# One rounding moved to ScalarE, a transpose of row maxima moved ahead of a score product, and a weight load moved to the end of its slot

## The chip, the cores and the metric

The kernel runs on one core of one Trainium2 chip. The metric is the device time of one execution in microseconds. A profiled execution also has a span, from the first to the last instruction of the program; times of the trace are counted from the start of that span.

## The reference

Attention with a decay, and behind it a soft mixture of experts. All numbers are float32.

```
q, k, v: (8 batches, 8 heads, 576, 64)   f: (8, 8, 576)
scores = q k^T / 8 + cum_i - cum_j,  cum = cumsum(log(clip(f)))
scores above the diagonal = -1e9;  scores -= max over the row
attn = exp(scores) / (sum + 1e-9);  x = attn v  -> (4608 tokens, 512)

logits = x phi (512 x 32);  d = softmax of logits over the tokens
slot_input = d^T x (32 x 512);  per expert (4 slots): relu(. w1[e]) w2[e]
out = softmax of logits over the slots @ slot_out   -> (4608, 512)
```

## The kernel before

**Heads and pairs.** The 64 heads are worked off in 32 pairs. Pair g has a slot of its own in the loop over g (lines 725 to 868). Its heads are h0 = 2g and h1 = 2g + 1. Four slots make a batch; w = (g - 4) mod 4 says which part of the soft-MoE work of an earlier batch a slot carries beside its own: logits behind slot w = 0, their exponentials and transposes in w = 1, the dispatch product and the first part of the combine weights in w = 2.

**Two passes over the scores.** Pass one (`s1`, L230, and `tops`, L243 to L249) computes scores with the query on the partitions, in float32r, in six products of a head (numbers 0 to 5) that lie in four banks. VectorE takes the maximum of every row from them into the tile `MT`: it reads the bank, adds the causal mask, and a second short instruction writes the maximum. Three PSUM banks rotate among these products. When all ten rows of a pair are in `MT`, `mturn` (L256) transposes them on TensorE into a free corner of the bank `pv[0]`, `mrows` copies them on ScalarE to a small tile `mr` (L265) and a DMA on SP's queue puts them as one more row into the rounded queries `YA` (L268). Pass two (`s2`, L283 and L284) computes the scores again with the key on the partitions, the row of maxima being part of the contraction. It is two products for each bank: the rounded operands `WA` and `YA`, and the rests of the rounding, `WB` and `YB`. ScalarE takes the exponential (`expo`, L290), GpSimd zeroes what lies above the diagonal (`causal`, L298 and L301), and `s3` (L315) multiplies with the values into `pv`. `norm` (L330 to L335) divides.

**Operands.** `load_qk` (L174) brings queries and keys of a pair to `RAW` (three buffers), `round_k` and `round_q` (L183, L188) round them on ScalarE into `WA` and `YA` (three buffers), `dup_k` and `dup_q` (L199, L203) copy the rounded ones by DMA into the other half of the partitions of `WB` and `YB` (two buffers), and GpSimd subtracts (`low_k` L209, `low_q` L214). `load_cum` (L194) brings two rows of cumulated decays into `WA`. `wload` (L128) loads one block of 512 KB of expert weights that stays in SBUF until the end.

**The slot.** In slot g, pass two works on pair g, while pass one works on head u0 = 2g + 3 (the second of pair g + 1) in the first half and u1 = 2g + 4 (the first of pair g + 2) in the second. So `MT` of pair g + 1 is complete once the maxima of u0's product 5 are in. The order on every engine is written out by hand: an engine takes its instructions in the order in which the program names them. In the second half of a slot that order is: `px` and `xcopy` of the fifth token block of pair g - 1 (a transposed output, copied from `pv[1]` on ScalarE, L372, two instructions), products 2 and 3 of u1 with their maxima, `s2` and `expo` of h1's banks 1 and 2, `mturn`, `mrows`, then the rest of pass one and two. SP's queue in a slot is: `load_qk`, `load_v`, `wload` (slots 2 to 28), the row of maxima, `load_cum`, `dup_q`, `dup_k`.

**The opening.** Lines 515 to 675 start pairs 0 and 1 by hand, with single products for pass one (`first`) and banks of pass two (`both`) interleaved. There one rounding, the queries of head 3, is made by VectorE (L625). `turner` is an identity; `warm` is a filler product on the constants. L578 is a memset on GpSimd of 64 columns of `YA` that the last product of a head's pass one reads.

```python
71  SIDES = [[x for n in zip(units(h, 0, range(4)), units(h, 1, range(4))) for x in n] ...]
256     nc.tensor.transpose(pm[0 : NBLK * (h1 - h0), 0:128].bitcast(F32R), MT[g % 3][...], turner)
265     nc.scalar.copy(mr[0:n], st["pm", g, h0][0:n, 0:128])
268     nc.sync.dma_start(dst.bitcast(F32), mr[0:n].bitcast(F32))
625 nc.vector.tensor_copy(YA[1][0:64, 1, 64:640], RAW[1][0:64, 1])
736 if 2 <= g < NRES + 2: wload(g - 2)
```

Of the kernel before, what the change touches and what calls it, by code (L numbers as in the profile page):

```python
# [20 lines left out]
NG = B * NPAIR  # L21
# [54 lines left out]
def attn_softmoe(ctx: ExitStack, tc: tile.TileContext, qk, v, f, phi, w1, w2, cst, out):  # L76
# [49 lines left out]
    def wload(n):  # L126
        i, q = divmod(ORDER[n], 4)
        nc.sync.dma_start(quarter[n], (w1, w2)[i % 2][i // 2][:, QW * q : QW * q + QW])  # L128
# [51 lines left out]
    def round_k(g, *hs):  # L180
        if pair(g):
            for h in hs or range(2):
                nc.scalar.copy(WA[g % 3][0:64, S * h : S * h + S], RAW[g % 3][64:128, h])  # L183

    def round_q(g, *hs):
        if pair(g):
            for h in hs or range(2):
                nc.scalar.copy(YA[g % 3][0:64, h, 64:640], RAW[g % 3][0:64, h])  # L188
# [45 lines left out]
    def tops(i, *which):  # L234
        if not head(i):
            return
        g, h = divmod(i, 2)
        for n in which:
            bank, o, blk, j0, w = TOPS[n]
            t = st["top", i % 2, bank]  # L240
            m0 = max(448 - (128 * blk + 64) + j0, 0)
            top = MT[g % 3][:, NBLK * h + blk : NBLK * h + blk + 1] if g else m2[h][:, blk, 1:2]
            if n == 2:  # L243
                nc.vector.tensor_reduce(top, t[:, o : o + w], axis=AX.X, op=ALU.max)  # L244
                continue
            nc.vector.tensor_tensor_reduce(  # L246
                out=t[:, o : o + w], in0=t[:, o : o + w], in1=mask[:, m0 : m0 + w], scale=1.0, scalar=top.bitcast(F32) if n == 3 else -3.0e38,
                op0=ALU.add, op1=ALU.max, accum_out=top,
            )  # L249

    def mturn(g, h0=0, h1=2):

        if not pair(g):
            return
        pm = pv[h0 and 1][:, 384:512]
        nc.tensor.transpose(pm[0 : NBLK * (h1 - h0), 0:128].bitcast(F32R), MT[g % 3][:, NBLK * h0 : NBLK * h1], turner)  # L256
        st["pm", g, h0] = pm
# [29 lines left out]
    def expo(i, bank):  # L287
        if head(i):
            t, at = st["bank"]
            nc.scalar.activation(PT[i % 2][:, SEG_O[bank] : SEG_O[bank] + at], t[:, 0:at], AF.Exp, scale=0.125)  # L290
# [20 lines left out]
    def s3(g, todo):  # L311
        for h, t, u, c in todo:
            r = queries(t, u)
            at = pt_col(c, 64 * r)
            nc.tensor.matmul(  # L315
                pvv[h][64 * u : 64 * u + 64, t, :], PT[h][:, at : at + 64], V[:, g % 2, c, 65 * h : 65 * h + 65], start=(c == 0), stop=(c == r // 2)
            )
# [47 lines left out]
    def xcopy(g, ts):  # L365
        if pair(g):
            n, o = TURN[ts[0]]
            to = XT[g % NPAIR]
            if ts == (4,):
                for h in range(2):  # L370
                    r = slice(64 * h, 64 * h + 64)
                    nc.scalar.copy(to[r, 128:192], pv[n][r, o + 64 * h : o + 64 * h + 64])  # L372
            elif ts == (0, 3):
                to = to[:, 0:384].rearrange("p (n c) -> p n c", c=192)[:, :, 0:128]
                nc.scalar.copy(to, pv[n][:, o : o + 256].rearrange("p (n c) -> p n c", c=128))
            else:
                nc.scalar.copy(to[:, PLACE[ts[0]] : PLACE[ts[0]] + 128 * len(ts)], pv[n][:, o : o + 128 * len(ts)])
# [221 lines left out]
    def first(i, n, busy=0):  # L599
        s1(i, *GROUPS[n])  # L600
        warm(busy, cs)
        tops(i, *GROUPS[n])

    def both(i, n):
        s2(i, *((0,), (1,), (2,), (3, 4, 5))[n])
        expo(i, n)
# [15 lines left out]
    both(0, 1)  # L622
    first(2, 0)
    both(0, 2)
    nc.vector.tensor_copy(YA[1][0:64, 1, 64:640], RAW[1][0:64, 1])  # L625
    next(r1)
    first(2, 1)
    next(r1)
    s2(0, 3, 4, 5)
    round_k(1, 1)  # L630
    expo(0, 3)
    dup_q(1, 1, 2)
    dup_k(1, 1, 2)
# [18 lines left out]
    first(3, 2)  # L652
    first(3, 3)
    round_k(2, 0)
    both(1, 3)
    causal(1)
    low_k(3)
    low_q(3)
    round_q(2, 0)
    s3(0, SIDES[0])  # L660
    mturn(1, 1, 2)
    mrows(1, 1, 2)
    first(4, 0)
    round_k(2, 1)
    round_q(2, 1)
    dup_q(2)
    dup_k(2)
    s3(0, LAST[0])
    norm(0)
    first(4, 1)  # L670
    s3(0, LAST[1] + SIDES[1][:8])
# [53 lines left out]
    for g in range(1, NG):  # L725
        h0, h1 = 2 * g, 2 * g + 1
        u0, u1 = h0 + 3, h0 + 4
        b, w = divmod(g - 4, NPAIR)
        c = b - 1 if w == 0 else b if (b, w) == (B - 2, 3) else None
        if g < 4:  # L730
            load_v(g + 1)
            load_qk(g + 3)
        else:
            load_qk(g + 3)
            load_v(g + 1)
        if 2 <= g < NRES + 2:
            wload(g - 2)
        if w == 1:
            weigh(b)
        low_q(h0 + 2)  # L740
        low_q(h1 + 2)
        s2(h0, 0)
        expo(h0, 0)
        norm(h0 - 1)
        if w == 1:
            mgroup(b)
        if w == 2:
            combine(b, 0)
        s1(u0, 2)
        tops(u0, 2)  # L750
        s2(h0, 1)
        expo(h0, 1)
        s1(u0, 3)
        tops(u0, 3)
        if 1 < g < NG - 1:
            px(g - 1, 0)
        s2(h0, 2)
        expo(h0, 2)
        if g == NG - 1:
            px(g - 1, 0)  # L760
        if g > 1:
            px(g - 1, 3)
        else:
            round_k(3, 0)
            round_q(3, 0)
        s1(u0, 0, 1)
        tops(u0, 0, 1)
        if g > 1:
            px(g - 1, 1)
        s2(h0, 3)  # L770
        if g > 1:
            xcopy(g - 1, (0, 3))
            px(g - 1, 2)
            xcopy(g - 1, (1, 2))
        s2(h0, 4)
        s1(u0, 4, 5)
        s2(h0, 5)
        expo(h0, 3)
        tops(u0, 4, 5)
        causal(h0)  # L780
        low_k(h0 + 2)
        if w == 1:
            mtop(b)
        s2(h1, 0)
        expo(h1, 0)
        if g == 1:
            for t in (0, 3, 1, 2):
                px(0, t)
        px(g - 1, 4)
        if g == 1:  # L790
            xcopy(0, (0, 3))
            xcopy(0, (1, 2))
        xcopy(g - 1, (4,))
        s1(u1, 2)
        tops(u1, 2)
        s2(h1, 1)
        expo(h1, 1)
        s1(u1, 3)
        tops(u1, 3)
        s2(h1, 2)  # L800
        if g < NG - 2:
            expo(h1, 2)
        mturn(g + 1)
        mrows(g + 1)
        if g >= NG - 2:
            expo(h1, 2)
        s1(u1, 0, 1)
        tops(u1, 0, 1)
        s2(h1, 3, 4)
        s1(u1, 4, 5)  # L810
        s2(h1, 5)
        expo(h1, 3)
        tops(u1, 4, 5)
        causal(h1)
        low_k(h1 + 2)
        if g == 1:
            round_k(3, 1)
            round_q(3, 1)
        load_cum(g + 3)
        dup_q(g + 2)  # L820
        dup_k(g + 2)
        if g == 29:
            sides[2].close()
            p2 = fresh(ctx, "p2", 2)
            wstream(*p2, RAW[30 % 3])
        if g == 30:
            sides[1].close()
            xp = ctx.enter_context(tc.tile_pool(name="xp", bufs=1))
            X.append(xp.tile([P, NBLK, 256], F32, name="X3"))
            p0 = fresh(ctx, "p0", 1)  # L830
            p1 = fresh(late, "p1", 3)
            wstream(*p0, *p1, RAW[31 % 3])
        if g == 31:
            sides[0].close()
            with tc.using_default_side("right"):
                tp = ctx.enter_context(tc.tile_pool(name="tp", bufs=1))
            cT = tp.tile([P, sum(CUT)], F32R, name="cT")
            wstream(tp.tile([P, QW], F32, name="w36"))
        if w == 1:
            mcast(b)  # L840
        if c is not None:
            combine(c, 1)
        if w == 2 and b < B - 2:
            dispatch(b, *range(NBLK))
        if g == NG - 1:
            st["lg", B - 1] = scratch(False, f"lg{B - 1}")
            nc.vector.memset(st["lg", B - 1][:, 128:192], -1.0e30)
        round_k(g + 3)
        if w == 1:
            weigh2(b)  # L850
            total(b)
        round_q(g + 3)
        if c is not None:
            combine(c, 2)
        s3(g, VALUES[:30])
        norm(h0)
        if g == 31:
            logits(B - 1, 0, 1)
            wstream(XTS[:, 0:QW], PTS[:, 0:QW])
            split(0, 0)  # L860
            split(1, 0)
        s3(g, VALUES[30:])
        if w == 0:
            logits(b, *range(NPAIR))
        if w == 1:
            tokens(b, 0, 1)
        if g == 28:
            wstream(RAW[29 % 3])
# [272 lines left out]
```

## Time and profile before

| | us |
|---|---|
| median of 3 runs | 391.46 |
| lowest and highest run | 390.41, 395.79 |
| profiled execution | 392.3 |
| its span | 390.6 |
| TensorE busy (matmuls) | 370.5, 95% |
| VectorE, ScalarE, GpSimd busy | 281.7, 271.3, 255.0 |

The profiled execution is 1.7 us longer than its span. TensorE's granted clock, over the whole span, was 0.984 of full speed. Busy matmul time is modelled from pipelined instructions, so ends of matmuls overlap; distances between their starts are read instead. A row of the timeline gives start, duration, engine, line, operation, tiles, and in brackets the idle time before it with what ended it; instructions that follow one another and are alike are merged (xN). A matrix product in float32 shows as two matmul records, one in float32r as one.

### The profile page before, as it was taken

Reading aid. Unit: us, or ns where it says so; the run is one execution under the profiler, and the core shown is the slowest. Engines: PE = TensorE matmul, PEld = TensorE weight load, DVE = VectorE, ACT = ScalarE, POOL = GpSimd, SP = SyncE. Lnnn points to the kernel's source line nnn. Section 1 sums busy time; section 2 is a strip of 40 time slices with the busy share of each in tenths; the row PEclk is TensorE's granted clock in tenths of the full one; section 3 lists DMA queues with packets and bytes.
Section 4 is the critical chain, followed back from the end, with each engine's and each line's share of the span. In section 5 each row is a group of like instructions: output and inputs, shape, how many; then the busy total and the mean of one; then the engine's idle time right before and its main releaser. Section 6 shows DMA issues by size and latency. Waiting matters only on the chain.

```text
span 390.6 us, 15123 instructions
## 1 busy us (share of the span) xinstructions
PE 370.5 (95%) x5863; PEld 330.7 (85%) x5863; DVE 281.7 (72%) x1080; ACT 271.3 (69%) x669; POOL 255.0 (65%) x357
## 2 busy tenths in 40 slices
PE   7999999999999999999999999999999998999870
PEld 7789999999999999999999999999999885567640
DVE  7978887878887788788878887878787534341681
ACT  8869887878787778787878787878786553021560
POOL 4897887878787878787878787878787821000000
PEclk9999999999999999999999999999999998999995
DMA  6875978777777777777777777777775899995798
GB/s 205 205 195 148 283 223 278 189 233 207 224 211 215 213 212 214 213 214 211 213 214 214 211 214 212 214 214 212 212 227 154 269 350 377 407 417 206 264 393 314
DMA packets 34344, 93.72 MB, mean 240 GB/s; under 512 B 4266, under 2 KB 8288, under 8 KB 34272
## 3 DMA queue, kind: packets, MB, share of 16 engines
q1 hardware_dynamic: 34272, 92.75, 76.4%
q8 instruction: 46, 0.75, 0.8%
q14 instruction: 26, 0.21, 0.2%
HBM read 63.93 MB, written 9.73 MB: 189 GB/s over the span
## 4 chain that ended last, share of the span: by engine, by line
PE 86%; DMA 6%; POOL 2%; DVE 1%; ACT 1%; issue 1%; POOLq 0%; DVEq 0%; ACTq 0%
PE pv L315 24%; PE ring L283 14%; PE s L230 13%; PE ring L284 13%; PE pv L342 5%; PE pv L981 4%; PE more L941 4%; PE lg L389 3%; DMA out<-RAW 3%; PE ds L475 2%; DMA YA<-mr 2%; DMA WB<-WA 1%; POOL WB L209 1%; DMA PTS<-in_f 1%; POOL YB L214 1%
## 5 line engine op out<-in xcount | busy, mean ns | idle before, releaser
L290 ACT ACTIVATE PTS<-ring 128x320 f32<-128x320 f32 (+2 forms) x256 | 118.1, 502 | 49.3 <-PE ring L284 36.4
L283 PE MATMUL ring<-YA,WA 67*128 67x320 f32 (+9 forms) x384 | 121.5, 330 | 0.8 <-DMA YA<-mr 0.8
L246 DVE CUSTOM_DVE_ANT_0 s<-s,mask 128x320 f32<-128x320 f32 (+3 forms) x256 | 109.0, 442 | 5.6 <-PE s L230 1.1
L284 PE MATMUL ring<-YB,WB 128*128 128x320 f32 (+4 forms) x384 | 110.4, 296 | 0.0
L315 PE MATMUL pv<-V,PTS 128*64 128x65 f32 x3200 | 101.9, 223 | 0.2 <-POOL WB L209 0.2
L315 PEld LDWEIGHTS pv<-V,PTS 128*64 128x64 f32 x3200 | 96.9, 138 | 3.1 <-issue 1.5
L230 PE MATMUL s<-WA,YA 66*128 66x288 f32 (+9 forms) x384 | 98.2, 310 | 0.8 <-DMA RAW<-in_qk 0.4
L209 POOL TENSOR_TENSOR WB<-RAW,WB 64x576 fp32r<-64x576 f32 x64 | 90.4, 1412 | 11.1 <-DMA WB<-WA 5.8
L214 POOL TENSOR_TENSOR YB<-RAW,YA 64x576 fp32r<-64x576 f32 x64 | 89.7, 1421 | 2.6 <-POOL EX L397 0.2
L283 PEld LDWEIGHTS ring<-YA,WA 67*128 67x128 f32 (+3 forms) x384 | 69.7, 183 | 6.3 <-issue 2.1
L284 PEld LDWEIGHTS ring<-YB,WB 128*128 128x128 f32 (+1 forms) x384 | 70.0, 182 | 0.1
L230 PEld LDWEIGHTS s<-WA,YA 66*128 66x128 f32 (+1 forms) x384 | 62.9, 190 | 7.4 <-ACT PTS L290 1.5
L301 POOL TENSOR_SCALAR_AFFINE_SELECT PTS<-PTS 128x128 f32<-128x128 f32 (+1 forms) x128 | 31.5, 268 | 21.1 <-ACT PTS L290 18.6
L246 DVE DVE_READ_ACCUMULATOR2_ANT MT<- 128x1 fp32r x310 | 43.8, 141 | 0.0
L298 POOL TENSOR_SCALAR_AFFINE_SELECT PTS<-PTS 128x384 f32<-128x384 f32 x64 | 33.5, 523 | 14.2 <-ACT PTS L290 10.3
L342 PE MATMUL pv<-cs,X 128*128 128x128 f32 x155 | 42.0, 277 | 0.0
L183 ACT CAST WA<-RAW 64x576 fp32r<-64x576 f32 x64 | 40.1, 668 | 1.0 <-DMA RAW<-in_qk 0.2
L188 ACT CAST YA<-RAW 64x576 fp32r<-64x576 f32 x63 | 39.6, 671 | 0.4
L246 DVE CUSTOM_DVE_ANT_0 s<-s,mask,MT 128x288 f32<-128x288 f32 x62 | 32.6, 526 | 9.3 <-PE s L230 0.4
L330 DVE TENSOR_SCALAR rl<-pv 128x5 f32<-128x5 f32 x64 | 10.5, 164 | 34.0 <-PE pv L315 23.6
L335 DVE TENSOR_TENSOR X<-pv,rl 128x320 f32<-128x320 f32 (+1 forms) x65 | 31.5, 486 | 2.4 <-DMA YA<-mr 0.3
L244 DVE TENSOR_REDUCE MT<-s 128x1 fp32r<-128x288 f32 x62 | 27.8, 449 | 0.4 <-PE s L230 0.4
(221 smaller groups left out, 389.2 us busy)
## 6 DMA issues: line engine op xcount, KB each, us to landing
w<-in_w SPq DMA_DIRECT2D x45, 512.0 KB
RAW<-in_qk SPq DMA_DIRECT2D x31, 576.0 KB
V<-in_v SPq DMA_DIRECT2D x32, 325.0 KB
YB<-YA SPq DMA_DIRECT2D x30, 288.0 KB
WB<-WA SPq DMA_DIRECT2D x30, 288.0 KB
p<-in_w SPq DMA_DIRECT2D x6, 512.0 KB
out<-RAW SPq DMA_DIRECT2D x6, 512.0 KB
out<-p SPq DMA_DIRECT2D x5, 512.0 KB
```

The source lines that it names most:

```text
L183: nc.scalar.copy(WA[g % 3][0:64, S * h : S * h + S], RAW[g % 3][64:128, h])
L188: nc.scalar.copy(YA[g % 3][0:64, h, 64:640], RAW[g % 3][0:64, h])
L209: nc.gpsimd.tensor_tensor(t[0:64], RAW[g % 3][64:128, h], t[64:128].bitcast(F32), op=ALU.subtract)
L214: nc.gpsimd.tensor_tensor(YB[g % 2][64:128, h], RAW[g % 3][0:64, h], YA[g % 3][0:64, h, 64:640].bitcast(F32), op=ALU.subtract)
L230: nc.tensor.matmul(t[:, o : o + w], ya[0:m, h, 128 * blk : 128 * blk + 128], wa[0:m, j0 : j0 + w], start=True, stop=True)
L246: nc.vector.tensor_tensor_reduce(out=t[:, o : o + w], in0=t[:, o : o + w], in1=mask[:, m0 : m0 + w], scale=1.0, scalar=top.bitcast(F32) if ...
L283: nc.tensor.matmul(o, wa[0:m, j0 : j0 + n], ya[0:m, h, 64 + i0 : 64 + i0 + w], start=True, stop=False)
L284: nc.tensor.matmul(o, wb[:, j0 : j0 + n], yb[:, h, i0 : i0 + w], start=False, stop=True)
L290: nc.scalar.activation(PT[i % 2][:, SEG_O[bank] : SEG_O[bank] + at], t[:, 0:at], AF.Exp, scale=0.125)
L298: nc.gpsimd.affine_select(d3, d3, pattern=[[0, 3], [1, 128]], compare_op=ALU.is_ge, fill=0.0, base=0, channel_multiplier=-1)
L315: nc.tensor.matmul(pvv[h][64 * u : 64 * u + 64, t, :], PT[h][:, at : at + 64], V[:, g % 2, c, 65 * h : 65 * h + 65], start=(c == 0), stop= ...
L342: nc.tensor.transpose(pm[:, 0:128], x[:, t, 128 * (p % 2) : 128 * (p % 2) + 128], ident)
```

## The change

1. In the opening, the rounding of head 3's queries moves from VectorE (L625) to ScalarE, as `round_q(1, 1)` behind `round_k(1, 1)` and ahead of an exponential.
2. In the opening, `round_q(2, 0)` moves on ScalarE ahead of the exponential of `both(1, 3)`. `first(4, 0)` moves ahead of the transposed maxima of head 3. The list `SIDES[0]` is cut at entry 20.
3. In the slots g > 1, `mturn` and `mrows` move ahead of `s2(h1, 2)` and its exponential. The copy of the fifth token block on ScalarE moves from behind `px` to behind `mrows`.
4. `wload` moves from the start of a slot, behind `load_qk` and `load_v`, to its end, behind `dup_q` and `dup_k`.

```diff
@@ opening
     both(0, 2)
-    nc.vector.tensor_copy(YA[1][0:64, 1, 64:640], RAW[1][0:64, 1])
     next(r1)
...
     round_k(1, 1)
+    round_q(1, 1)
     expo(0, 3)
...
     round_k(2, 0)
+    round_q(2, 0)
     both(1, 3)
     causal(1)
     low_k(3)
     low_q(3)
-    round_q(2, 0)
-    s3(0, SIDES[0])
+    s3(0, SIDES[0][:20])
+    first(4, 0)
     mturn(1, 1, 2)
     mrows(1, 1, 2)
-    first(4, 0)
...
-    s3(0, LAST[0])
+    s3(0, SIDES[0][20:] + LAST[0])
@@ slot g
-        if 2 <= g < NRES + 2:
-            wload(g - 2)
...
-        xcopy(g - 1, (4,))
+        if g == 1:
+            xcopy(0, (4,))
         s1(u1, 2)
         tops(u1, 2)
         s2(h1, 1)
         expo(h1, 1)
         s1(u1, 3)
         tops(u1, 3)
+        if g > 1:
+            mturn(g + 1)
+            mrows(g + 1)
+            xcopy(g - 1, (4,))
         s2(h1, 2)
-        if g < NG - 2:
-            expo(h1, 2)
-        mturn(g + 1)
-        mrows(g + 1)
-        if g >= NG - 2:
-            expo(h1, 2)
+        expo(h1, 2)
+        if g == 1:
+            mturn(g + 1)
+            mrows(g + 1)
         s1(u1, 0, 1)
...
         dup_q(g + 2)
         dup_k(g + 2)
+        if 2 <= g < NRES + 2:
+            wload(g - 2)
```

## Rows read from the trace of the kernel before

**Rows 1.** Page, part 1: busy time, share of the span, instructions.

```profile
PE 370.5 (95%) x5863; PEld 330.7 (85%) x5863; DVE 281.7 (72%) x1080; ACT 271.3 (69%) x669; POOL 255.0 (65%) x357
```

**Rows 2.** Stretches: length, busy time of PE, PEld, DVE, ACT, POOL, clock, DMA share, GB/s.

```profile
35.57:121.00 85.43, 85.36 (x1450) 80.47 (x1447) 67.87 (x270) 68.96 (x170) 70.74 (x96) 1.00 0.77 223
130.30:303.60 173.30, 173.09 (x2936) 162.31 (x2937) 138.99 (x556) 136.19 (x341) 139.09 (x191) 1.00 0.74 213
```

**Rows 3.** Waits of TensorE: total us, times, longest.

```profile
PE ring L283 <- DMA YA<-mr: 0.8, 2, 0.5
```

**Rows 4.** Chain of waits, 109 to 131 us: start, us, what.

```profile
126.45 3.80 DMA YA<-mr
```

**Rows 5.** Timeline of VectorE, the opening.

```profile
6.52 0.46 DVE L557 CAST PTS<-PTS 64x576 fp32r<-64x576 f32 x1
...
15.43 1.32 DVE L625 CAST YA<-RAW 64x576 fp32r<-64x576 f32 x1
...
18.61 0.14 DVE L246 DVE_READ_ACCUMULATOR2_ANT MT<- 128x1 fp32r x1
```

**Rows 6.** Timeline of TensorE, the opening.

```profile
16.94 0.30 PE L230 MATMUL s<-WA,YA 66*128 66x64 f32 x1 [0.37 <-DMA RAW<-in_qk]
...
18.13 0.49 PE L511 MATMUL ring<-cs 128*128 128x192 f32 x2
18.89 0.22 PE L256 MATMUL pv<-turner,MT 128*5 128x128 f32 x1 [0.28 <-POOL WB L209]
```

**Rows 7.** Timeline of GpSimd, the opening.

```profile
15.01 1.42 POOL L214 TENSOR_TENSOR YB<-RAW,YA 64x576 fp32r<-64x576 f32 x1
16.49 0.54 POOL L578 MEMSET YA<- 64x128 f32 x2
```

**Rows 8.** Timeline of ScalarE, the opening.

```profile
16.09 0.67 ACT L183 CAST WA<-RAW 64x576 fp32r<-64x576 f32 x1
...
17.82 0.94 ACT L290 ACTIVATE PTS<-ring 128x448 f32<-128x448 f32 x2 [0.57 <-ACT PTS L290]
```

**Rows 9.** Timeline of VectorE: last maximum of u0 in slots 6, 11 and 26.

```profile
76.62 0.14 DVE L246 DVE_READ_ACCUMULATOR2_ANT MT<- 128x1 fp32r x1
...
124.86 0.14 DVE L246 DVE_READ_ACCUMULATOR2_ANT MT<- 128x1 fp32r x1
...
269.50 0.14 DVE L246 DVE_READ_ACCUMULATOR2_ANT MT<- 128x1 fp32r x1
```

**Rows 10.** Timeline of TensorE: h1's bank 2 in the same slots, and a transpose.

```profile
76.62 0.31 PE L283 MATMUL ring<-YA,WA 98*128 98x320 f32 x1
...
125.07 0.31 PE L283 MATMUL ring<-YA,WA 67*128 67x320 f32 x1
...
269.40 0.31 PE L283 MATMUL ring<-YA,WA 67*128 67x320 f32 x1
269.55 0.31 PE L284 MATMUL ring<-YB,WB 128*128 128x320 f32 x1
269.70 0.23 PE L256 MATMUL pv<-turner,MT 128*10 128x128 f32 x1
```

**Rows 11.** Timeline of ScalarE, slot 11, around the copy of the maxima.

```profile
125.10 0.42 ACT L372 COPY XTS<-pv 64x64 f32<-64x64 f32 x2
125.54 0.77 ACT L290 ACTIVATE PTS<-ring 128x320 f32<-128x320 f32 x2
126.19 0.24 ACT L265 CAST mr<-pv 10x128 fp32r<-10x128 f32 x1
```

**Rows 12.** Timeline of SP's queue: two loads of queries and keys.

```profile
38.37 0.39 SPq L174 DMA_DIRECT2D RAW<-in_qk  x1
...
54.09 0.54 SPq L174 DMA_DIRECT2D RAW<-in_qk  x1
```

**Rows 13.** Timeline of ScalarE: the roundings of those loads, and what follows one.

```profile
42.21 1.24 ACT L183 CAST WA<-RAW 64x576 fp32r<-64x576 f32 x2 [0.18 <-DMA RAW<-in_qk]
...
45.08 0.87 ACT L290 ACTIVATE PTS<-ring 128x448 f32<-128x448 f32 x2 [0.37 <-PE ring L284]
...
59.60 1.24 ACT L183 CAST WA<-RAW 64x576 fp32r<-64x576 f32 x2
```

## The prediction

> **What bounds the kernel now.** I read the page's busy times first: TensorE is busy for 95% of the span, the next engine for 72% [rows 1]. An average may hide a stage with room, so next come the stretches: in 35.57 to 121 us TensorE is busy for 85.36 of 85.43 us, in 130.3 to 303.6 us for 173.09 of 173.30, at full clock, while the DMA engines are at three quarters [rows 2]. In the slots, then, a wait of another engine is worth nothing, and one put on TensorE is paid in full. Third, TensorE's list of waits: for the row of maxima it waits twice, 0.8 us together, the longer 0.5 [rows 3]; the chain of waits shows that one behind a DMA which took 3.80 us from its issue in slot 11 [rows 4]. Outside the opening and the tail, 0.8 us is all that an earlier row of maxima can win. The rest had to be found in the order of single instructions, so the timelines of the opening and of the slots' middles come last.
>
> **Part 1 and 2, the opening.** VectorE's copy takes 1.32 us, and its maxima go on behind it, until the last one of head 2 is written at 18.75 (18.61 + 0.14) [rows 5]. TensorE's transpose of these maxima starts at 18.89, behind two fillers from 18.13, after 0.28 us of idle time [rows 6]. The page puts that to GpSimd, but the maxima, written 0.14 us before, explain it as well and are what the transpose reads. Ends of matmuls are modelled: 0.31 us long records follow each other at 0.15 in a stream [rows 10], so the real stall is nearer 0.28 + 0.16 = 0.44. Without the copy the maxima come up to 1.3 us sooner, bounded by the 64-column product at 16.94 (its end 17.24 plus a maximum, under 18.0), and the stall goes: -0.44. ScalarE pays 0.67 for it, behind the rounding at 16.09; its idle 0.57 before 17.82 takes most [rows 8], 0.10 is passed on to the exponentials, whose banks the filler product reuses. Next is the wait at 16.94, 0.37 us [rows 6]: the memset of the columns that this product reads runs from 16.49 on GpSimd, which is in a row of subtractions that the change doesn't touch [rows 7]. It stays.
> I take -0.4. The ends: -0.8 if the 0.37 goes too, +0.7 if the whole rounding on ScalarE shows.
> `round_q(2, 0)` ahead of an exponential delays that by 0.67; the values product that needs it stands 20 entries later, so 0. The list cut at 20 has just 20 entries: nothing moves between its parts. Only `first(4, 0)` and the transpose change places; both are TensorE's and both needed, 0.
>
> On the port the Trainium skill speaks too ("GPSIMD Engine Reference", Specifications): GpSimd shares its SBUF interface with VectorE, and contends with two-port VectorE modes. By it the copy would have slowed GpSimd, and removing it would bring the memset sooner. The trace shows VectorE slowed (1.32 us, where a like cast at 6.52 took 0.46 [rows 5]), but GpSimd's subtraction beside it not (1.42 us [rows 7]). That is rival 2.
>
> **Part 3, the transpose one product sooner.** What it wins: in slot 11 the copy of the maxima starts at 126.19 on ScalarE, behind two copies of the fifth block (from 125.10) and two exponentials (from 125.54) [rows 11]. With the block copies and one exponential behind it, it starts some 0.6 sooner (0.44 by the copies, the rest by the exponential). The DMA's 3.80 us then end 0.6 earlier and the 0.5 wait is gone: -0.5. The other wait (0.3) is in slot 30, where the same edit costs as much (below).
> What it costs: TensorE works in its program's order, so a transpose that has to wait for VectorE holds all behind it. Before, `s2(h1, 2)` covered that. In slot 26 the last maximum is written at 269.64 (269.50 + 0.14) [rows 9], and the transpose starts at 269.70, 0.06 later [rows 10]: just ready, with no idle time. In the new order it would stand where `s2(h1, 2)` starts now, at 269.40, and still can't start before 269.70: a stall of 0.30. In slot 6 the maximum is there at 76.76, plus 0.06 against a place at 76.62: 0.20. Slot 11 is an ordinary one: 125.00 + 0.06 against 125.07: 0.00 [rows 9, 10]. Which slots are which follows from VectorE's queue: in w = 2 `combine` step 0 (L495, L496) stands ahead of the maxima and makes them late. These are slots 6, 10, 14, 18, 22 and 26: 0.20 + 5 x 0.30 = +1.7. The late 0.3 isn't won back: from there to the slot's end the chain holds nothing but TensorE.
> In the 22 ordinary slots the transpose is ready just at its place; the weight load behind it may come later: between 0 and 0.06 each, 0 to +1.3. I take 0.01 each, +0.2, as the transposes that are just ready now show no idle time. Slot 30 is a w = 2 slot too: +0.3 and the wait of 0.3 fall together, 0.
> The exponential of h1's bank 2 moves behind one maxima copy (0.24) and the block copies (0.42) and no longer behind those ahead of it: about 0.4 later. `causal(h1)` needs it, and GpSimd is busy with `low_k` until then; cover gone, 0.4 late at the values product's second half, which starts 1.2 us after the first. 0.
>
> **Part 4, the weights.** SP's issue of 0.4 us is passed by nothing urgent: the row of maxima waits for ScalarE, not for SP. What changes is the order of the data: 512 KB now stand ahead of the queries and keys of the same slot (26 loads) instead of behind. At 223 GB/s for a share of 0.77 [rows 2] a full queue moves 290 GB/s, and 512 KB are 1.8 us. The only rounding that waited for its load began 3.8 us after the issue (38.37 to 42.21); the shortest other distance I found is 5.5 us (54.09 to 59.60) [rows 12, 13]. 3.8 + 1.8 = 5.6: 0.1 us late in one slot, under ScalarE's idle 0.37 behind such roundings [rows 13]. I take 0; the ends are 0 and rival 3.
>
> **Sum.** -0.4 - 0.5 + 1.7 + 0.2 = +1.0 us. The profiled execution, 392.3 us (span 390.6 and 1.7 around it), would become 393.3; it stands 0.8 above the median of 391.46, which becomes **392.5 us**. With the ends of the terms that case spans 391.1 (opening -0.8, ordinary slots 0) to 394.7 (opening +0.7, ordinary slots +1.3).
>
> **Rivals.**
> 1. The transposes don't stall. VectorE's maxima would have to come 0.3 us sooner in the w = 2 slots. For: a VectorE that waits for TensorE elsewhere could catch up when the opening gives it time. Against: the same delay in slots 10 to 26, and nothing taken from VectorE's slots. Then -0.4 - 0.5 and 0: 390.6 us.
> 2. GpSimd's port: without the copy the memset comes sooner by the 0.37 that TensorE waits. Against: the subtraction of 1.42. Then +0.6: 392.1 us.
> 3. Slower: the queries and keys behind the weights come late, ScalarE stands at `round_k` with the next slot's exponentials behind it, and TensorE runs out of free banks. It decides where a load takes over 5.5 - 1.8 = 3.7 us now; the one measured took 3.8 at most. If landing in a full queue takes 2 us more than that, some ten slots wait 0.5 or so past ScalarE's idle time: +5, 397.5 us. All 26 by 0.5 or more: +13, 405 us. For: one rounding waits already. Against: one only, of 32.
> 4. The change does nothing that shows: the transpose is late whenever it could help, and the stalls and gains cancel: 391.5 us.
>
> **How the numbers follow.** My forecast 0.5; rival 1 0.2; rival 2 0.05; rival 3 0.15, of which 0.03 beyond 2%; rival 4 0.1. The runs before spread over 1.4%, so 2% (7.8 us) is about what can be told from no change: faster 0.01, within 2% 0.95, slower 0.04. The range reaches from rival 1 to the upper end of the forecast and the low part of rival 3: 390.0 to 395.0.
>
> **What would show it.** Right: TensorE waits for VectorE at L256 in slots 6 to 26 of w = 2, some 0.3 each; those slots 0.3 longer, the others unchanged; no wait for the row of maxima in slot 11; slot 2 starts 0.4 earlier than 35.57 [rows 2]. Wrong: ScalarE waiting at L183 for a DMA in many slots, no wait at L256, or a slot 2 that starts later.

## The result

Over 22 runs each, taken in the same rounds, the kernel before had a median of 390.94 us (389.62 to 395.97) and the changed one 393.42 us (393.04 to 395.36). The ratio is 1.0079, with a 95% interval of 1.0066 to 1.0092: the change costs 2.6 to 3.6 us, about 3.1. The ratio is of fast runs alone and so leaves out two slow ones of the kernel before, 395.79 and 395.97; the medians of all runs are 2.48 apart. The forecast was 392.5 us in a range of 390.0 to 395.0, by a sum of +1.0 us. The time lies in the range and on the forecast's side; the cost is about three times the sum.

### The profile page after: what moved, and what is told of

It is laid out like the page before. It is cut to its first block, busy times and chain, and to the rows that moved or that the text cites. A ratio compares the mean times of both kernels' runs of the same rounds, so it can differ in the third digit from the quotient of the medians.

```text
span 391.5 us, 15170 instructions
## 1 busy us (share of the span) xinstructions
PE 371.3 (95%) x5863; PEld 329.3 (84%) x5863; DVE 281.2 (72%) x1079; ACT 275.4 (70%) x670; POOL 254.8 (65%) x357
## 4 chain that ended last, share of the span: by engine, by line
PE 75%; DVE 9%; ACT 6%; DMA 5%; issue 2%; POOL 0%; SPq 0%; ACTq 0%; DVEq 0%; POOLq 0%
PE pv L315 21%; PE ring L283 12%; PE ring L284 10%; PE s L230 10%; DVE s L246 4%; PE pv L342 4%; PE pv L984 4%; PE more L944 4%; PE lg L389 3%; DMA out<-RAW 3%; PE ds L475 2%; ACT WA L183 2%; ACT YA L188 2%; DMA WB<-WA 1%; PE pv L256 1%
## 5 line engine op out<-in xcount | busy, mean ns | idle before, releaser
L290 ACT ACTIVATE PTS<-ring 128x320 f32<-128x320 f32 (+2 forms) x256 | 119.7, 502 | 45.9 <-PE ring L284 35.0
L283 PE MATMUL ring<-YA,WA 67*128 67x320 f32 (+9 forms) x384 | 123.1, 334 | 0.0
L230 PE MATMUL s<-WA,YA 66*128 66x288 f32 (+9 forms) x384 | 96.0, 306 | 1.1 <-ACT YA L188 0.4
L283 PEld LDWEIGHTS ring<-YA,WA 67*128 67x128 f32 (+3 forms) x384 | 69.7, 183 | 5.1 <-issue 2.1
L230 PEld LDWEIGHTS s<-WA,YA 66*128 66x128 f32 (+1 forms) x384 | 64.0, 190 | 6.3 <-ACT PTS L290 1.9
L342 PE MATMUL pv<-cs,X 128*128 128x128 f32 x155 | 42.1, 278 | 0.1
L330 DVE TENSOR_SCALAR rl<-pv 128x5 f32<-128x5 f32 x64 | 10.5, 164 | 36.6 <-PE pv L315 27.0
L335 DVE TENSOR_TENSOR X<-pv,rl 128x320 f32<-128x320 f32 (+1 forms) x65 | 31.5, 486 | 2.4 <-DMA V<-in_v 0.3
```

The lines of the kernel that those rows point to most:

```text
L230: nc.tensor.matmul(t[:, o : o + w], ya[0:m, h, 128 * blk : 128 * blk + 128], wa[0:m, j0 : j0 + w], start=True, stop=True)
L283: nc.tensor.matmul(o, wa[0:m, j0 : j0 + n], ya[0:m, h, 64 + i0 : 64 + i0 + w], start=True, stop=False)
L342: nc.tensor.transpose(pm[:, 0:128], x[:, t, 128 * (p % 2) : 128 * (p % 2) + 128], ident)
```

## The profile after

The profiled execution of the changed kernel took 393.22 us (span 391.5), only 0.9 more than that of before. So the stretches come first. Both fences have one row for slots 2 to 10, one for slots 12 to 29 and one from slot 31 to the end (length, busy time of TensorE, its weight loads, VectorE, ScalarE, GpSimd, TensorE's granted clock, DMA share, GB/s). The changed kernel:

```profile
34.87:121.53 86.66, 86.13 (x1449) 80.24 (x1446) 68.02 (x270) 69.98 (x170) 70.67 (x96) 1.00 0.76 215
130.37:306.12 175.75, 174.72 (x2941) 162.14 (x2937) 139.66 (x557) 138.53 (x342) 139.67 (x191) 1.00 0.74 214
314.55:391.48 76.93, 61.23 (x859) 41.89 (x855) 33.69 (x104) 25.72 (x74) 4.61 (x15) 0.94 0.92 348
```

The kernel before, from its own starts of the same slots:

```profile
35.57:120.96 85.39, 85.32 (x1449) 80.43 (x1447) 67.87 (x270) 68.96 (x170) 70.70 (x96) 1.00 0.77 223
130.30:303.62 173.32, 173.11 (x2937) 162.33 (x2937) 139.01 (x556) 136.19 (x341) 139.11 (x191) 1.00 0.74 213
312.28:390.57 78.29, 62.26 (x855) 42.80 (x855) 33.28 (x102) 25.60 (x74) 4.61 (x15) 0.92 0.90 341
```

The slots are longer: 86.66 against 85.39 us and 175.75 against 173.32, at the same clock. TensorE's idle time in them grew from 0.07 to 0.53 and from 0.21 to 1.03; where [rows 2] had TensorE busy without a gap there are gaps now, and the rest of the loss lies under records whose ends are modelled. Slots 2 to 30 together take 279.68 instead of 276.71 us: **+2.97**. The opening ends 0.70 sooner (slot 2 starts at 34.87, not 35.57), and what follows slot 31 is 1.36 shorter. +2.97 - 0.70 - 1.36 = +0.91, the difference of the spans. The last two terms belong to these two executions, as the second profile of the kernel before shows below; the change is in the slots' term, in which single slots scatter too (in that second profile the same slots take 277.09).

What TensorE and its weight loads wait for in the slots now (total us, times, longest):

```profile
PEld pv L256 <- DVE MT L246: 3.0, 7, 0.7
PEld pv L342 <- DVE X L335: 2.4, 14, 0.4
PEld pv L256 <- DVE row L414: 1.3, 7, 0.2
```

Of these three rows the profile of before has only the first, once and with 0.2 us; the wait of [rows 3] for the row of maxima is gone. The first is the stall that was forecast at the transpose: six of its seven waits, 0.38 to 0.39 each, are in slots 6, 10, 14, 18, 22 and 26, the seventh, 0.65, is in slot 30. Slot 10 shows one (VectorE, then TensorE: start, us, what):

```profile
115.44 0.14 DVE L246 DVE_READ_ACCUMULATOR2_ANT MT<- 128x1 fp32r x1
```

```profile
115.20 0.30 PE L230 MATMUL s<-WA,YA 97*128 97x288 f32 x1
115.64 0.22 PE L256 MATMUL pv<-turner,MT 128*10 128x128 f32 x1
115.70 0.38 PE L283 MATMUL ring<-YA,WA 67*128 67x320 f32 x1
```

The last maximum is written at 115.58 and the transpose starts 0.06 later, as in [rows 10]; the product before it started at 115.20, and in a stream of full speed the next would have started some 0.14 later. The chain of waits says the same in another way: in this slot it leaves TensorE and runs through VectorE's queue to the transpose (start, us, what):

```profile
111.99 0.34 DVE sm L495
...
112.35 0.33 DVE ctok L496
112.67 0.38 DVE MT L244
...
115.29 0.23 DVE s L246
115.53 0.07 DVE MT L246
115.59 0.04 issue
115.64 0.22 PE pv L256
```

At its head stand L495 and L496, which the prediction named as what makes the maxima late in the w = 2 slots.

The second row, 14 waits of TensorE's weight load at L342 for `X`, was forecast nowhere. L342 multiplies the normalized result of the pair before, `X`, which VectorE writes in `norm` (L330 to L335) at the head of a slot. What is seen of the norm's first instruction in the changed kernel (kind, count, ns min/median/max, first and last start in us; the second row is the wait instruction):

```profile
L330 DVE TENSOR_SCALAR rl<-pv x64: 152/165/168, 22.9 to 323.0; 128x5 f32<-128x5 f32 x64
L330 DVEq EVENT_SEMAPHORE  x49: 21/21/21, 22.8 to 314.7; - x49
```

and before:

```profile
L330 DVE TENSOR_SCALAR rl<-pv x64: 152/165/167, 23.6 to 320.6; 128x5 f32<-128x5 f32 x64
L330 DVEq EVENT_SEMAPHORE  x26: 21/21/21, 23.5 to 310.7; - x26
```

So 49 of the 64 norms, 23 more than before, now have a separate wait instruction on VectorE's queue ahead of them. In the trace of before, the norm of h1 at the head of the w = 3 and w = 0 slots waits for one semaphore, which TensorE's instructions raise; in the changed kernel it waits for that and for a second one, which ScalarE's raise.

The second wait goes with the place of the fifth-block copies (L372), as e1 and e2 show below: behind the row copy they give the norm this wait, at their old place they don't. In slot 11 of the changed kernel those copies had ended 5.2 us before the norm began, but the wait is still executed. The rows of slot 11 (all engines: start, us, what, and the idle time before), before:

```profile
120.96 0.47 PE L283 MATMUL ring<-YA,WA 67*128 67x448 f32 x1
...
121.08 0.16 DVE L330 TENSOR_SCALAR rl<-pv 128x5 f32<-128x5 f32 x1 [0.20 <-PE pv L315]
...
121.50 0.49 DVE L335 TENSOR_TENSOR X<-pv,rl 128x320 f32<-128x320 f32 x1
...
122.05 0.32 PE L342 MATMUL pv<-cs,X 128*128 128x128 f32 x1
```

and after:

```profile
121.53 0.47 PE L283 MATMUL ring<-YA,WA 67*128 67x448 f32 x1
...
121.72 0.17 DVE L330 TENSOR_SCALAR rl<-pv 128x5 f32<-128x5 f32 x1 [0.27 <-PE pv L315]
...
122.15 0.49 DVE L335 TENSOR_TENSOR X<-pv,rl 128x320 f32<-128x320 f32 x1
...
122.69 0.14 PEld L342 LDWEIGHTS pv<-cs,X 128*128 128x128 f32 x1 [0.15 <-DVE X L335]
122.69 0.33 PE L342 MATMUL pv<-cs,X 128*128 128x128 f32 x1
```

The norm starts 0.19 us after the slot instead of 0.12, and L342, which reads what it makes, 1.16 instead of 1.09. `X` was just ready before (written at 121.99, read at 122.05); now the weight load waits for it, and the 0.07 is handed on to TensorE in full.

## The experiments

All slots' lengths in one table, worked out from the timelines: the start of a slot's first L283 to that of the next one's. Medians over slots 6 to 29 by w, then the single slots that vary, and slots 2 to 30 together (us).

```
                      w=2    w=3    w=0    w=1   slot 1 at  slot 2  slot 11  slot 30  2 to 30
before               10.23   8.76  10.19   9.26    26.30     8.74    9.34     8.66    276.71
after                10.60   8.84  10.28   9.31    25.61     8.75    8.83     8.43    279.68
e1_copies_back       10.60   8.77  10.22   9.31    25.60     8.74    8.77     8.39    278.71
e2_turn_back         10.26   8.84  10.27   9.23    25.74     9.48    8.82     8.40    277.78
e3_slots_back        10.27   8.78  10.20   9.24    25.58     9.27    8.77     8.29    277.03
e4_opening_only      10.25   8.76  10.21   9.25    26.00     8.74    9.27     8.67    276.63
e5_turn_only         10.60   8.84  10.27   9.30    25.58     8.75    8.83     8.83    280.12
e6_weights_only      10.26   8.75  10.20   9.24    25.71     8.76    8.77     8.31    275.85
e7_old_in_w2         10.30   8.84  10.28   9.31    25.60     8.74    8.84     8.31    277.68
e8_row_first         10.26   8.75  10.21   9.24    25.65     8.75    8.76     8.30    275.93
e9_before_again      10.26   8.76  10.21   9.25    25.82     9.55    8.77     8.79    277.09
e10_opening_again    10.26   8.77  10.21   9.25    25.68     8.75    8.92     8.29    275.95
e11_weights_again    10.26   8.77  10.20   9.25    26.66     8.73    9.19     8.66    277.52
e12_row_first_again  10.25   8.77  10.21   9.24    25.62     9.02    8.77     8.33    276.10
```

Theory A of the first four runs: part 3 is the whole loss, by the transpose in the w = 2 slots and by the late copies in the others. The medians of the kernel before beside them were 390.45 (e1 to e4), 390.93 (e5 to e8) and 390.38 us (e9 to e12).

**e1, the changed kernel with the fifth-block copies at their old place.**

```diff
-        if g == 1:
-            xcopy(0, (4,))
+        xcopy(g - 1, (4,))
         ...
-            xcopy(g - 1, (4,))
```

> The changed kernel, with the two copies of the fifth token block (L372) back ahead of product 2 of u1; the transpose and the row copy stay early. Theory A (two costs: TensorE held at the early transpose in the w = 2 slots, and VectorE's division of h1, L330, which now has to wait for ScalarE too, 0.07 us each, in front of a transpose of X that TensorE needs at once): the slots w = 3 and w = 0 get back 0.07 each (8.84 to 8.77, 10.28 to 10.21), the slots w = 2 stay at 10.6; 0.9 us faster than the changed kernel, about 1.6 to 2.2 slower than the kernel before. Theory B (the early transpose costs in every slot): nothing changes, 2.5 to 3.1 slower than before.

392.34 us, 1.0053 of before (1.0033 to 1.0073). The w = 3 and w = 0 slots are back at 8.77 and 10.22, the w = 2 and w = 1 slots stay. The norm has its 26 separate waits again (the same row as above, of e1):

```profile
L330 DVEq EVENT_SEMAPHORE  x26: 21/21/21, 22.8 to 312.5; - x26
```

The copies' place costs 0.97 us of slots.

**e2, the changed kernel with the transpose behind h1's third product again.** `s2(h1, 2)` goes ahead of `mturn`, `mrows` and `xcopy`, and nothing else changes.

> The changed kernel, with the transpose of the maxima back behind h1's bank 2, but the row copy and the fifth block's copies still ahead of that bank's exponential. Theory A: the slots w = 2 lose their 0.3 of waiting for the last maximum (10.60 to 10.3), six of them, 2.0 us together; w = 3 and w = 0 keep their 0.07; 0.5 to 1.1 slower than the kernel before. Theory B (the early transpose costs in every slot): all slots are as before, 0.7 to 1.2 faster than the kernel before.

391.01 us, 1.0017 (1.0003 to 1.0030). The mirror image: w = 2 at 10.26 and w = 1 at 9.23, while w = 3 and w = 0 keep 8.84 and 10.27 and the norm its 49 waits. TensorE's waits in e2 hold the one kind and hardly the other:

```profile
PEld pv L342 <- DVE X L335: 2.3, 13, 0.4
...
PEld pv L256 <- DVE MT L246: 0.2, 1, 0.2
```

Slot 2 took 9.48, 0.74 more than before; e9 says what to make of that.

**e3 and e4, part 3 undone, and the opening alone.** e3 is the changed kernel with the old middle of a slot (opening and weights stay); e4 is the kernel before with the new opening.

> The changed kernel with its third part undone: the opening and the weights as changed, the middle of the slot as before. Theory A: all of the loss is in the middle of the slots, so the slots are 8.75, 10.2, 9.26, 10.24 as before and the opening's 0.7 us is left: 0.5 to 0.8 faster than the kernel before. Rival (the weights ahead of queries and keys cost time too): no faster than the kernel before, with idle time of ScalarE at L183 in many slots.

> The kernel before with the changed opening alone. Theory A: slot 2 starts 0.7 us sooner (34.87 instead of 35.57) and nothing else moves: 0.7 us faster than the kernel before; the same as the run with the weights moved too, within 0.2. If the weights cost time, this one is faster than that by as much.

e3: 390.86 us, 1.0002 (0.9988 to 1.0016); e4: 390.31 us, 0.9998 (0.9978 to 1.0017). All classes of slots are those of before, so the loss is part 3's. Both were expected to be 0.5 to 0.8 us faster than the kernel before; no gain of the opening could be measured in either.

**e5, part 3 alone; e6, part 4 alone.**

```diff
 # e5: before, with the middle of a slot as in the changed kernel
 # e6: before, with
-        if 2 <= g < NRES + 2:
-            wload(g - 2)
         ...
         dup_k(g + 2)
+        if 2 <= g < NRES + 2:
+            wload(g - 2)
```

> The kernel before with part 3 alone: the transpose, the row copy and the fifth-block copies stand ahead of h1's third score product; opening and weights as before. Theory A (part 3 is the whole loss: the early transpose stalls TensorE by about 0.35 us in each w = 2 slot, and the norm that waits for ScalarE's late copies costs about 0.07 in each w = 3 and w = 0 slot): w = 2 slots 10.60 us, w = 3 slots 8.84, w = 0 slots 10.28, slots 2 to 30 together 279.5 to 279.9 (before 276.7), 393.2 to 393.8 us, that is 1.006 to 1.009 of before. Theory B (the weights at the slot's end cost a part of it, through later queries and keys): under 1.005 of before, and slots 2 to 30 below 279.0.

> The kernel before with part 4 alone: a slot's weights are issued at its end, behind the doubled operands. Theory A (the weights are worth nothing): 390.2 to 390.9 us, 0.999 to 1.001 of before; slots as before, but slots 2 and 5 up to 0.5 us longer, as in the kernel with part 3 undone, where ScalarE waited for the queries and keys there. Theory B (later queries and keys cost time): 391.3 us or more, over 1.002. Theory C (the moved weights spare the stage behind the slots): slot 31 to the end 1 us shorter, and 389.5 us or less.

e5: 394.55 us of 6 runs, 1.0103 (1.0082 to 1.0124), slots +3.41. It is somewhat more than expected (slot 30 alone is 0.40 longer than in the changed kernel) and holds all of the loss. e6: 391.01 us, 1.0010 (0.9997 to 1.0024): nothing, though its profiled execution, 389.56 us, was the lowest of its 12 runs and had the shortest slots of all kernels.

**e7, the new order only outside the w = 2 slots.** `if g > 1 and w != 2:` ahead of the moved lines, and the same lines behind `s2(h1, 2)` for w == 2.

> The changed kernel, but in the w = 2 slots the transpose, the row copy and the fifth-block copies stand behind h1's third score product again. Theory A (seven or eight w = 2 slots lose 0.3 to 0.35 each at the transpose): w = 2 slots 10.25 us, w = 3 and w = 0 slots unchanged at 8.84 and 10.28, slots 2 to 30 together 277.3 to 277.8, time 2.0 to 2.4 below the changed kernel: 391.0 to 391.4 us. Theory B (the transpose's stall is only passed on to another wait in these slots): w = 2 slots stay above 10.45, and the time stays above 392.3.

Slots 277.68 us, inside what was expected, with w = 2 at 10.30: the stall is 0.30 a slot, and it goes. Of the waits, the transposes' is gone and L342's stays:

```profile
PEld pv L342 <- DVE X L335: 2.4, 14, 0.3
...
PEld pv L256 <- DVE MT L246: 0.3, 1, 0.3
```

The time, 391.91 us (1.0026, 1.0009 to 1.0044), is 1.5 below the changed kernel, by the ratios 2.1, and 0.5 above the expectation.

**e8, the row copy ahead of one exponential, all else at its old place but the opening.**

```diff
         s2(h1, 2)
-        if g < NG - 2:
+        if g == 1:
             expo(h1, 2)
         mturn(g + 1)
         mrows(g + 1)
-        if g >= NG - 2:
+        if g > 1:
             expo(h1, 2)
```

> The opening of the changed kernel; in the slots the transpose stays behind h1's third score product and the fifth-block copies at their place, but the row copy goes ahead of that product's exponential on ScalarE; weights as before. Theory A: the wait for the row of maxima in slot 11 shrinks from 0.5 to 0.1 or less, since the copy starts some 0.25 to 0.3 earlier and the DMA behind it as much, no slot gets longer than before by over 0.03, slots 2 to 30 together 276.2 to 276.7 us, and with 0.3 to 0.7 from the opening 389.7 to 390.2 us, 0.998 to 0.9995 of before. Theory B (the later exponential holds up the masks and the values product): w = 2 and w = 3 slots 0.05 to 0.1 longer, slots 2 to 30 at 277.5 or more, and no gain.

389.72 us, 0.9987 (0.9963 to 1.0011), slots 275.93, no class of slots longer.

**e9 to e12, second profiles.** The profiles of before, e4 and e6 disagreed with each other in terms of 0.3 to 0.9 us, so the kernel before, the opening alone, the weights alone and the row copy alone were profiled again.

> The kernel before, unchanged, for a second profile. Theory A (in the profile of before, the wait of 0.37 us in the opening belongs to that one execution, and the wait of 0.5 in slot 11 belongs to the kernel): slot 1 starts at 25.6 to 25.7 us instead of 26.30, slot 11 is 9.2 to 9.4 us long again, slots 2 to 30 together 276.5 to 276.8. Theory B (both belong to the kernel): slot 1 starts at 26.2 or later, slot 11 as in A. Theory C (both belong to one execution): slot 11 takes 8.75 to 8.8 us.

> The kernel before with the new opening alone, a second profile. Theory A (the new opening wins the transpose's 0.28 to 0.44 us and gives 0.4 back where TensorE waits for ScalarE's rounding, so it is worth nothing): slot 1 starts at 25.6 to 25.7 us, TensorE waits 0.4 for the rounded queries at 17.5, slot 11 takes 9.2 to 9.4. Theory B (it wins what the profile of before had as a stall): slot 1 starts 0.3 us or more before that of the second profile of the kernel before.

> The kernel before with part 4 alone, a second profile, since the first was the fastest of its 12 runs. Theory A (the moved weights free the row of maxima in slots 11 and 30, 0.5 and 0.3 us, and give as much back in most executions where queries and keys come late): slot 11 8.75 to 8.8, slot 30 8.3 to 8.4, and one or two of the slots 2 to 6 longer by 0.3 to 0.6; slots 2 to 30 together 276.2 to 277.0. Theory B (they only win): slots 2 to 30 at 275.7 to 276.0 again.

> The new opening, and the row copy ahead of the third exponential with the transpose, the block copies and the weights at their old places, timed again for a narrower interval. Theory A (it wins the waits for the row of maxima, 0.8 us, and loses nothing): 0.997 to 0.9995 of before, slots 2 to 30 together 275.8 to 276.1. Theory B (the gain of the first profile belonged to that execution): 0.9995 to 1.002 of before.

e9 is nearest to theory C. The unchanged kernel took 390.9 us; slot 1 starts at 25.82 without the wait at 16.94, and slot 11 takes 8.77, **without the wait for the row of maxima** on which the prediction had put 0.5 us; instead slot 2 takes 9.55 and slot 30 8.79. e10 (389.69 us) has its slot 1 and its wait for the rounding where theory A put them, but slot 11 at 8.92. e11 (392.2 us) bore out neither of its theories: it swings by 1.7 us of slots against e6, the same kernel, with these waits:

```profile
ACT WA L183 <- DMA RAW<-in_qk: 7.2, 9, 1.8
...
PE ring L283 <- DMA YA<-mr: 0.7, 2, 0.3
```

So waits for a DMA that lands late come and go between executions of one kernel. With the row copy at its old place on ScalarE, TensorE waited for the row in four of seven profiles: before 0.8 us, e4 0.7, e9 0.4, e11 0.7, but not in e3, e6 and e10. With an earlier one (after, e1, e2, e5, e7, e8, e12) its products did so in none of seven, though its weight loads still waited for the row twice in e1 and once in e2, 0.2 to 0.3 us each (and once in e10). The earlier copy makes this wait rarer; that it ends it is not shown. e12: 389.98 us, 0.9990 (0.9975 to 1.0004), slots 276.10. The ratio lies in theory A's bounds, but its interval holds 1. This best kernel, 3.4 to 3.7 us below the changed one, cannot be told from the kernel before.

The end differs between executions too. Two stretches late in the run, the kernel before in its first profile:

```profile
326.00:328.00 2.00, 1.19 (x12) 0.65 (x15) 1.43 (x5) 0.78 (x5) 0.00 (x0) 0.77 0.97 324
328.00:330.00 2.00, 2.00 (x41) 1.51 (x34) 0.00 (x0) 0.11 (x1) 0.00 (x0) 0.50 1.01 385
```

and in e9:

```profile
326.00:328.00 2.00, 1.18 (x30) 0.90 (x33) 1.44 (x5) 0.79 (x4) 0.00 (x0) 1.00 1.02 408
328.00:330.00 2.00, 1.72 (x34) 1.16 (x27) 0.85 (x4) 0.77 (x4) 0.56 (x2) 1.00 1.03 422
```

In the first of the two stretches TensorE is busy for 1.19 and 1.18 of 2.00 us, and in both executions it stands idle there for 0.81 to 0.82 us ahead of the same product (L711). In one its clock falls to 1.2 GHz 0.06 us after that product's start (0.77, then 0.50), in the other it stays at 2.4. From slot 31 to the end that is 78.29 against 76.99 us. Of all 14 profiles three have this fall (before, e4, e7: 78.26 to 78.32 us), the others take 76.93 to 77.07. With e9's end in place of the first one, the 1.36 us that the changed kernel seemed to win there are 0.06.

## Why the prediction was right in its sign and short in its size

That the time lies only 0.9 us from the forecast is in part luck: the forecast stood on a median of 391.46 from three runs, 0.52 above that of the 22. Of the sum itself, +1.0 against about +3.1, the terms came out like this. (Its lower end is added up wrongly: -0.8 - 0.5 + 1.7 is +0.4, which gives 391.9, not 391.1. Nothing else rests on it.)

- **The transpose, +1.7:** right, and somewhat small. Slots 6, 10, 14, 18, 22 and 26 grew by 0.31, 0.36, 0.34, 0.37, 0.38 and 0.40: 2.16. e7 takes 0.30 a slot of it out, which was the forecast price of one. The rest, 0.06 a slot, is nearly gone in e2 (10.26) and not in e7 (10.30); where it arises is not shown.
- **The ordinary slots, +0.2: the step that failed.** "In the 22 ordinary slots the transpose is ready just at its place; the weight load behind it may come later: between 0 and 0.06 each [...] I take 0.01 each". They cost 0.50 (w = 3 without slot 11), 0.80 (w = 0) and 0.27 (w = 1): 1.57. The step looked for the cost at the moved transpose alone. It was there in the w = 1 slots (the third wait row; 9.31 against 9.26, gone in e2). But the larger part came from the copies that moved along: they gave a later reader of their bank, the norm, a second semaphore to wait for, and 0.07 us of that on VectorE reached TensorE through L342 (e1 against e2). The prediction had priced the copies only by what they move in ScalarE's own order. Some 0.2 of the w = 0 sum is slot 8 alone, 10.46 to 10.64 us in the four kernels with the late copies (after, e2, e5, e7) and 10.18 to 10.22 in the others. In three of them VectorE pauses 0.2 us between L330 and L331 there, for nothing that the trace shows; the cause stays open.
- **Slot 11, -0.5:** the mechanism is right: the copy starts at 126.16, 4.63 us into the slot and not 5.23, the forecast 0.6 sooner, and the wait is gone. Its size is not the kernel's: in e9 there was no wait in slot 11 to win.
- **Slot 30, 0:** -0.23 in these profiles, within what one kernel scatters there (e4 and e10: 8.67 and 8.29).
- **The opening, -0.4:** between these two executions slot 1 starts 0.69 sooner, but the gain depends on where GpSimd stands. The stall at the transpose, which the prediction had found, is gone; but TensorE now waits for ScalarE's rounding, of which the prediction had passed on 0.10, and to the exponentials only:

```profile
17.49 0.50 PE L230 MATMUL s<-WA,YA 66*128 66x320 f32 x2 [0.39 <-ACT YA L188]
```

Where GpSimd is on time (its memset, L578, starts at 15.4 to 16.0), the one pays for the other: old openings start slot 1 at 25.58, 25.71 and 25.82, new ones at 25.58 to 25.74. Where GpSimd is late (memset at 16.49 to 16.86), old ones start it at 26.30 and 26.66, a new one (e4) at 26.00.
- **The weights, 0:** right as far as e6's time can tell (0.1 us faster to 0.9 slower). Rival 3 (queries and keys late) did not come in the changed kernel's profile, where ScalarE waits once for such a load, 1.1 us. Its onset is seen in others with the weights moved: ScalarE waits 9 times in e3, e6 and e11, 7.0, 5.6 and 7.2 us. Most of that lies beside TensorE's work, but perhaps not all: right behind ScalarE's longest waits, 1.75 to 1.82 us in slot 4 of e1, e3 and e11, slot 5 took 9.54 to 9.64 us, and 9.23 to 9.30 in the other eleven profiles. The order in time is all that ties the two.
- **Rival 1** (the transposes do not stall) fell with the first wait row, **rival 4** with the ratio. **Rival 2** (the copy holds up GpSimd's memset) held by half. The prediction ruled it out by the subtraction; what the copy lengthens is the memset itself. In e11 (with the copy) and e4 (without it) GpSimd is equally late:

```profile
16.84 0.54 POOL L578 MEMSET YA<- 64x128 f32 x2
```

```profile
16.86 0.34 POOL L578 MEMSET YA<- 64x128 f32 x2
```

The 64-column product of [rows 6] starts at 17.29 in e11 and at 17.11 in e4: about half of the rival's 0.37 us is the copy's. The rest goes with how late GpSimd's row is in an execution; in e9, where it is on time, the product does not wait at all.

The sum with measured sizes, +2.16 + 1.57 - 0.51 - 0.23 + 0.01 for slot 2, is +3.00 for the slots, but for rounding the 2.97 seen, and +3.1 by the ratio. Against the slots of e9 the changed kernel's are 2.59 longer.

## What to carry to other kernels

Moving an instruction in a queue worked off in order has a price at two ends: at its new place, where its input may not be there yet, and at every later reader of the buffers that it or what moves with it touches, which may need to wait for one more semaphore. On the path of an engine that is busy without a gap, 0.07 us in 14 slots costs as much as three visible stalls of 0.3. And a wait of half a microsecond for a DMA in one profile is not yet a property of the kernel: where a forecast rests on it, look whether a second execution has it.

## What the hardware showed that was not expected

VectorE's copy of the old opening (L625, 64x576) took 1.32 us before and in other executions of the same lines 1.33, 0.77, 0.53 and 0.52. What decides is GpSimd's subtraction. In e6 the copy and the subtraction that it overlaps (VectorE, then GpSimd):

```profile
15.39 0.77 DVE L625 CAST YA<-RAW 64x576 fp32r<-64x576 f32 x1
```

```profile
14.43 1.42 POOL L214 TENSOR_TENSOR YB<-RAW,YA 64x576 fp32r<-64x576 f32 x1
```

The subtraction ends at 15.85 and the copy at 16.16, 0.31 later. Before, [rows 5, 7] give 16.43 and 16.75, 0.32 later; in e11 0.30. In e5, where the subtraction was over before the copy began, the copy takes 0.53. So the copy does not run slower beside GpSimd: it stands until GpSimd is done, and the subtraction is as long as ever (1.40 to 1.43). The Trainium skill says so ("SBUF — State Buffer", SBUF: two separate sides): of a VectorE operation that uses the shared port pair and a GpSimd one, whichever starts first holds it for its whole instruction and the other is blocked. These rows agree. It held the other way round too: the first of the two memsets, begun while the copy ran, took 0.40 us instead of 0.20 and ended 0.14 to 0.15 after the copy in all four executions (before, e6, e9, e11). In e5 copy and memset began 0.02 us apart, the copy first, and there the memset ran through in 0.20; so recorded starts that close do not tell which one holds.

A wait for a second semaphore that has long been reached held up VectorE's next instruction by 0.07 us (0.19 against 0.12 after the slot's start), though the wait instruction itself is recorded with 21 ns.
